# A prompt kernel (state-space convolution and SwiGLU FFN): the buffers of the FFN's inner rows are moved by 64 bytes

## The chip, the cores and the metric

The kernel runs on one core of a Trainium2 chip. The metric is device time of one execution in microseconds. A core has engines that run side by side: PE multiplies matrices (its weight loads are shown as PEld), ACT evaluates functions and copies, DVE and POOL work element by element, SP issues transfers. Each has its own queue of instructions, and semaphores tie the queues together. All operands of PE lie in the core's on-chip memory of 128 partitions; an address below means the byte offset within a partition.

## The reference

The input is a prompt of L = 2048 tokens with D = 448 channels. A conditioning vector gives six rows of scale, shift and gate. Two residual branches follow each other: a diagonal state-space convolution along the tokens, and a SwiGLU FFN with F = 1792 inner rows.

```python
mod = (_silu(c) @ w_mod).reshape(c.shape[0], 6, 1, -1)
sa, ca, ga, sb, cb, gb = ...
h = _layernorm(x) * (1 + ca) + sa
x = x + ga * ssm_conv(h, A, B, C, log_dt, Dskip)
h = _layernorm(x) * (1 + cb) + sb
x = x + gb * ((_silu(h @ w_gate) * (h @ w_up)) @ w_down)
```

Everything is float32, and the FFN is nearly all of the arithmetic: 2048 x 448 x 1792 x 3 products.

## The kernel before

The tokens are 16 tiles of 128. They are handled in six blocks of 2, 2, 3, 3, 3 and 3 tiles (`BLOCKS`). The FFN's inner rows are 14 groups of 128, called `f` in the code. A first stage of about 33 us loads and prepares the six rows, the scan's coefficients and the first two tiles. From then on the FFN of one block runs while the scan and the second normalisation of the next block are worked in between (`TIMES` says at which `f`).

PE multiplies in a one-pass form of float32 that keeps fewer bits. To keep the precision, each operand is split into a high part and a low part, and three products are added: high x high, high x low, low x high. So each tensor of the FFN exists twice: `hhi` and `hlo` for the normalised input (channels on partitions, four slices of the 448 channels), the slices 0 to 6 of `gu` for the gate and up weights, `phi` and `plo` (in the code `hi` and `lo`) for the inner rows, and `wdh` and `wdl` for the down weights.

For one `f`, `gate_up` issues 22 matmuls (line 754): for gate and for up, seven with `hhi` and four with `hlo`. Here a 128 x 128 piece of the weights `gu` is loaded into the array, and `hhi` or `hlo` streams through it, 256 or 384 columns, by the block's number of tiles. ACT makes silu of the gate into a buffer `p` (line 769), DVE multiplies it with the up result (784), ACT copies the product to `phi` (791), and DVE writes what is left of it to `plo` (792).

`down` (line 804) belongs to the `f` before. Here the roles are turned round: a 128 x 128 piece of `phi` or `plo`, one tile of tokens, is the weights that are loaded, and `wdh` or `wdl` streams, 448 columns. For each of three products and each tile of the block there is one matmul: nine with three tiles, six with two. So PE's program is, without end, 22 gate/up matmuls and 9 or 6 down matmuls. Now and then come three matmuls of the scan (lines 976 to 978), which load the triangular matrix `tri` and stream `vh`, `v1` and `vl`, 448 columns too. In the last block the last two inner rows are multiplied in another order (line 832).

Where the buffers lie is set by their order and sizes alone, each pool taking the next free place. The pool `hid` is the last one. It has two buffers of each name, first two of `p`, then of `phi`, then of `plo`, and it ends 224 bytes below the end of the memory. In this layout `hhi`, `hlo`, all `gu`, `wdh`, `wdl`, `p`, `phi` and `plo` start at 32 modulo 256, and `tri` at 128 modulo 256. Their slices keep that, since a slice of 128 columns is 512 bytes, and a row of 448 columns is 7 x 256 bytes. One exception is written into the code: in a block of two tiles, the columns of `hhi` and `hlo` that are used begin at column 48, 192 bytes further on.

```python
first_col = lambda n: 48 if n == 256 else 0
```

Only the first block (`fresh`) takes `p` from the pool `hid`; later blocks use two pieces of a buffer that is free by then (`p_of`).

Of the kernel before, what the change touches and what calls it, by code (L numbers as in the profile page):

```python
# [8 lines left out]
F32 = mybir.dt.float32  # L9
# [42 lines left out]
def f32(ap):  # L52
    return ap.bitcast(F32)
# [3 lines left out]
def tile_kernel(ctx, tc, x, a_re, a_im, b_re, b_im, c_re, c_im, log_dt,  # L57
# [13 lines left out]
    def bank():  # L71
        t = psg.tile([128, 512], F32, name="bank")
        return t
# [26 lines left out]
    p_of = [spare[:, q * 512:q * 512 + MB * 128] for q in range(2)]  # L100
# [11 lines left out]
    def split_d(j, part=None):  # L112
        hi, lo = wp[j]
        if not part:
            sc.copy(hi, wdn[j])
        if part != 0:
            ve.tensor_tensor(lo, wdn[j], f32(hi), op=OP.subtract)

    def split_w(j, part):
        w = raw[j]  # L120
        if part == 0:
            sc.copy(wgu[j][:, :, 0:3, :], w[:, :, 0:3, :])  # L122
            sc.activation(wgu[j][:, :, 3, :], w[:, :, 3, :], AF.Copy, scale=half)  # L123
        else:
            ve.tensor_tensor(wgu[j][:, :, 3:7, :], w[:, :, ::-1, :], f32(wgu[j][:, :, 0:4, :][:, :, ::-1, :]), op=OP.subtract)  # L125
# [604 lines left out]
    def run_blocks(pools, stages, first=None):  # L730
        work, hid = pools.work, pools.hid
        def ffn(ts, fresh, last, todo):
# [4 lines left out]
            def gate_up(f, nw):  # L737
                head = fresh and f < 2
                if fresh and f:
                    split_d(f)  # L740
                w = wgu[f]
                p = hid.tile([128, 256], F32, name="p") if fresh else p_of[f % 2]
                hi = hid.tile([128, MB * 128], F32R, name="phi")
                lo = hid.tile([128, MB * 128], F32R, name="plo")
                ps = [bank(), bank()]

                top = [(k, a) for k, ws in enumerate(((0, 6), (1, 5), (2, 4), (3,))) for a in ws]
                low = [(k, k) for k in range(4)]  # L750

                def mm(s, ka, lo, first=False, end=False):
                    for q, (k, a) in enumerate(ka):
                        pe.matmul(ps[s][:, 0:n], w[:, s, a], (hlo if lo else hhi)[:, k, first_col(n):first_col(n) + n],  # L754
                                  start=first and q == 0, stop=end and q == len(ka) - 1)

                if head:
                    for k in range(3):
                        for s in range(2):
                            mm(s, [(k, k)], False, k == 0)  # L760
                    for s in range(2):
                        mm(s, [(k, 6 - k) for k in range(3)] + [(3, 3)], False)
                    for s in range(2):
                        mm(s, low, True, False, True)
                else:
                    for s in range(2):
                        mm(s, top, False, True)
                        mm(s, low, True, False, True)
                sc.activation(p[:, 0:n], ps[0][:, 0:n], AF.Silu)  # L769
                for g, a in todo.get((f, 2), []):  # L770
                    g(*a)
                pp[f] = hi, lo
                if last and f == NF - 1:
                    c_ = [slice(q * 128, (q + 1) * 128) for q in range(len(ts))]
                    for q in range(len(ts) + 1):
                        for o in c_[q:q + 1]:
                            ve.tensor_tensor(ps[1][:, o], p[:, o], ps[1][:, o], op=OP.mult)  # L777
                            sc.copy(hi[:, o], ps[1][:, o])
                        for o in c_[max(q - 1, 0):q]:
                            ve.tensor_tensor(lo[:, o], ps[1][:, o], f32(hi[:, o]), op=OP.subtract)  # L780
                    return
                if nw is not None:
                    split_w(nw, 0)
                ve.tensor_tensor(ps[1][:, 0:n], p[:, 0:n], ps[1][:, 0:n], op=OP.mult)  # L784
                if fresh and f == 0:
                    split_d(0, 1)
                    for g, a in todo.get("mid", []):
                        g(*a)
                elif nw is not None:
                    split_w(nw, 1)  # L790
                sc.copy(hi[:, 0:n], ps[1][:, 0:n])  # L791
                ve.tensor_tensor(lo[:, 0:n], ps[1][:, 0:n], f32(hi[:, 0:n]), op=OP.subtract)  # L792
                if fresh and f == 0:
                    split_w(nw, 1)
# [52 lines left out]
            for f in range(NF):  # L847
                gate_up(f, f + 2 if fresh and f + 2 < NF else None)
                if fresh:
                    pools.load(f + 2 + NS, f + NS)  # L850
                if last and f in (2, 4):
                    gated(NF - 2 + (f == 4))
                for g, a in todo.get((f, 0), []):
                    g(*a)
                if f and not (last and f == NF - 1):
                    down(f - 1, qz)
                if last and f == NF - 2:
                    last_sums()
                for g, a in todo.get((f, 1), []):
                    g(*a)  # L860
# [250 lines left out]
```

## Time and profile before

| | us |
|---|---|
| median of three runs | 474.72 (474.66 to 474.8) |
| the profiled execution | 474.99 |
| its span, first to last instruction | 473.1 |
| PE busy | 464.2 |
| PEld busy | 439.3 |
| DVE busy | 282.6 |
| ACT busy | 160.1 |
| PE busy in the gate/up matmuls, line 754 (hhi / hlo) | 209.2 / 130.6 |
| PE busy in the down matmuls, line 804 (three products) | 58.0 / 58.1 / 58.2 |

The busy time of matmuls is that of their union: a matmul is shown from its start until its last result is written, the next one starts before that, and the overlap is counted once, for one of them. What a matmul costs on PE is therefore read as the distance from its start to the start of the next, in the timeline. There a row is a run of equal instructions: start, length, engine, line, what it writes and reads, the size of the loaded weights, the size of what streams, and how many. A distance is the difference of two rows' starts divided by the count of the first. Starts are given to 0.01 us, so that a distance over nine matmuls is known to about 1 ns and a single one to 10 ns.

### The profile page before, as it was taken

The numbers are of one execution on the slowest core, as the hardware profiler recorded it, in microseconds if no ns is written. First come the engines' busy times: TensorE is split into PE (matmuls) and PEld (weight loads), VectorE is DVE, ScalarE is ACT, GpSimd is POOL, SyncE is SP. The second block draws the span as 40 slices with busy tenths as digits, with TensorE's granted clock in tenths as the row PEclk, the third lists the DMA queues.
The fourth block names the chain that finished last, engine by engine and source line by source line (L and its number), as shares of the span: only waits on it lengthen the run. The fifth ranks groups of instructions, "written<-read, shape, count | busy, mean of one in ns | idle before, by whom it ended". The sixth has DMA issues, their size and how long they took to land.

```text
span 473.1 us, 7027 instructions
## 1 busy us (share of the span) xinstructions
PE 464.2 (98%) x2735; PEld 439.3 (93%) x2735; DVE 282.6 (60%) x540; ACT 160.1 (34%) x359; POOL 62.4 (13%) x88
## 2 busy tenths in 40 slices
PE   6999999999999999999999999999999999999995
PEld 4669999999999999999999999999999999999995
DVE  5888999778865547573744756464666553222125
ACT  5879566522243122233212233321223222221111
POOL 1222001000000224100022410004141000000000
PEclk9999999999999999999999999999999999999999
DMA  8966652110003000111300011130000112000001
GB/s 307 405 245 183 211 177 92 58 40 2 2 0 99 0 1 0 46 45 46 116 2 0 2 45 46 44 118 1 1 22 24 46 44 79 22 1 1 1 0 64
DMA packets 18779, 31.24 MB, mean 66 GB/s; under 512 B 2608, under 2 KB 13488, under 8 KB 18736
## 3 DMA queue, kind: packets, MB, share of 16 engines
q1 hardware_dynamic: 18096, 30.53, 18.8%
q8 instruction: 23, 0.38, 0.4%
q10 hardware_dynamic: 640, 0.18, 0.2%
q14 instruction: 20, 0.16, 0.1%
HBM read 24.61 MB, written 6.03 MB: 65 GB/s over the span
## 4 chain that ended last, share of the span: by engine, by line
PE 95%; DMA 3%; DVE 1%; ACT 0%; SPq 0%; issue 0%; DVEq 0%
PE bank L754 60%; PE dn L804 28%; DMA wm<-in_w_mod_groups_dram 2%; DMA x<-in_A_u_dram 1%; PE dn L476 1%; PE bank L256 1%; PE bank L977 1%; PE cv L976 1%; PE cv L978 1%; PE bank L266 0%; DVE x L843 0%; PE bank L227 0%; PE bank L394 0%; PE cv L989 0%; PE bank L397 0%; DVE bank L777 0%
## 5 line engine op out<-in xcount | busy, mean ns | idle before, releaser
L754 PE MATMUL bank<-hhi,gu 128*128 128x384 f32 (+1 forms) x1176 | 209.2, 317 | 0.2 <-issue 0.2
L754 PEld LDWEIGHTS bank<-hhi,gu 128*128 128x128 f32 x1176 | 189.8, 188 | 3.8 <-issue 1.0
L754 PE MATMUL bank<-hlo,gu 128*128 128x384 f32 (+1 forms) x672 | 130.6, 316 | 0.0
L754 PEld LDWEIGHTS bank<-hlo,gu 128*128 128x128 f32 x672 | 109.1, 188 | 0.2
L784 DVE TENSOR_TENSOR bank<-raw,bank 128x384 f32<-128x384 f32 (+1 forms) x69 | 36.8, 534 | 121.2 <-PE bank L754 118.5
L791 ACT CAST phi<-bank 128x384 fp32r<-128x384 f32 (+1 forms) x83 | 36.8, 443 | 138.3 <-DVE bank L784 138.2
L769 ACT ACTIVATE raw<-bank 128x384 f32<-128x384 f32 (+1 forms) x70 | 32.9, 470 | 122.7 <-PE bank L754 113.8
L792 DVE TENSOR_TENSOR plo<-bank,phi 128x384 fp32r<-128x384 f32 (+1 forms) x83 | 42.4, 511 | 37.6 <-ACT phi L791 37.5
L804 PE MATMUL dn<-wdh,plo 128*128 128x448 f32 x218 | 58.2, 368 | 0.0
L804 PE MATMUL dn<-wdl,phi 128*128 128x448 f32 x218 | 58.1, 367 | 0.0
L804 PE MATMUL dn<-wdh,phi 128*128 128x448 f32 x218 | 58.0, 367 | 0.0
L804 PEld LDWEIGHTS dn<-wdl,phi 128*128 128x128 f32 x218 | 40.9, 188 | 3.9
L804 PEld LDWEIGHTS dn<-wdh,plo 128*128 128x128 f32 x218 | 40.9, 188 | 3.9
L804 PEld LDWEIGHTS dn<-wdh,phi 128*128 128x128 f32 x218 | 38.5, 188 | 1.1
L185 POOL TENSOR_SCALAR rsb<-mvb 128x1 f32<-128x1 f32 (+2 forms) x13 | 4.6, 354 | 143.6 <-DVE mvb L157 143.6
L125 DVE TENSOR_TENSOR gu<-raw,gu 128x1024 fp32r<-128x1024 f32 x14 | 17.0, 1218 | 1.2 <-ACT gu L123 1.2
L185 POOL TENSOR_SCALAR rsa<-mva 128x3 f32<-128x3 f32 (+1 forms) x6 | 2.3, 380 | 99.3 <-DVE mva L157 97.0
L951 POOL TENSOR_TENSOR m<-m,gm 128x448 f32<-128x448 f32 x9 | 10.4, 1150 | 21.1 <-DVE m L202 17.4
L965 DVE TENSOR_TENSOR vl<-m,vh 128x448 fp32r<-128x448 f32 x12 | 9.0, 754 | 6.7 <-ACT vh L964 6.1
L122 ACT CAST gu<-raw 128x768 fp32r<-128x768 f32 x14 | 11.7, 832 | 0.0
L970 POOL TENSOR_TENSOR m<-m,gd 128x448 f32<-128x448 f32 x9 | 11.5, 1281 | 0.0
L215 ACT ACTIVATE raw<-raw,rsb 128x64 f32<-128x64 f32 x14 | 4.8, 346 | 18.9 <-DVE raw L212 9.7
(243 smaller groups left out, 412.0 us busy)
## 6 DMA issues: line engine op xcount, KB each, us to landing
raw<-in_B_w_gate_up_dram SPq DMA_DIRECT2D x14, 512.0 KB, 3.7
rawd<-in_B_w_down_dram SPq DMA_DIRECT2D x16, 224.0 KB, 3.9
x<-in_A_u_dram SPq DMA_DIRECT2D x12, 224.0 KB, 3.0
out_dram<-x SPq DMA_DIRECT2D x11, 224.0 KB, 1.9
xd<-raw SPq DMA_DIRECT2D x9, 256.0 KB, 2.0
raw<-xd SPq DMA_DIRECT2D x36, 64.0 KB, 2.0
wm<-in_w_mod_groups_dram SPq DMA_DIRECT2D x5, 448.0 KB, 8.2
wm<-in_w_mod_groups_dram SPq DMA_DIRECT2D x5, 336.0 KB, 8.2
```

Source lines behind the costliest of these rows:

```text
L122: sc.copy(wgu[j][:, :, 0:3, :], w[:, :, 0:3, :])
L125: ve.tensor_tensor(wgu[j][:, :, 3:7, :], w[:, :, ::-1, :], f32(wgu[j][:, :, 0:4, :][:, :, ::-1, :]), op=OP.subtract)
L185: po.tensor_scalar(rs[:, 0:n], self.mv[:, 0:n, 1], EPS, None, op0=OP.add)
L754: pe.matmul(ps[s][:, 0:n], w[:, s, a], (hlo if lo else hhi)[:, k, first_col(n):first_col(n) + n], start=first and q == 0, stop=end and q = ...
L769: sc.activation(p[:, 0:n], ps[0][:, 0:n], AF.Silu)
L784: ve.tensor_tensor(ps[1][:, 0:n], p[:, 0:n], ps[1][:, 0:n], op=OP.mult)
L791: sc.copy(hi[:, 0:n], ps[1][:, 0:n])
L792: ve.tensor_tensor(lo[:, 0:n], ps[1][:, 0:n], f32(hi[:, 0:n]), op=OP.subtract)
L804: pe.matmul(dn[q][:, 0:D], u[:, cs], v, start=f == 0 and z == 0, stop=f == (NF - 3 if last else NF - 1) and z == 2)
L951: (ve if on_v else po).tensor_tensor(v, h, g, op=OP.mult)
L965: ve.tensor_tensor(vl, v0, f32(vh), op=OP.subtract)
L970: (ve if on_v else po).tensor_tensor(h, h, gd, op=OP.mult)
```

## The change

In the first block's `gate_up`, the buffer `p` is asked for with 264 columns in place of 256.

```diff
                 w = wgu[f]
-                p = hid.tile([128, 256], F32, name="p") if fresh else p_of[f % 2]
+                p = hid.tile([128, 264], F32, name="p") if fresh else p_of[f % 2]
                 hi = hid.tile([128, MB * 128], F32R, name="phi")
                 lo = hid.tile([128, MB * 128], F32R, name="plo")
```

The additional eight columns are used by nothing. Each of the two buffers `p` grows from 1024 to 1056 bytes, so the second `p` starts 32 bytes later, and the two `phi` and the two `plo` start 64 bytes later: at 96 modulo 256, with `wdh` and `wdl` still at 32. This holds for every block, since `phi` and `plo` are the same buffers throughout. No other buffer moves, and each engine's instructions and waits stand in the same order as before.

## The prediction

> **What bounds the kernel now.** I read the page's busy lines first, then the chain that ended last, then the waits of PE, and only then the timeline of PE at a few places in the middle.
>
> ```profile
> span 473.1 us, 7027 instructions
> PE 464.2 (98%) x2735; PEld 439.3 (93%) x2735; DVE 282.6 (60%) x540; ACT 160.1 (34%) x359; POOL 62.4 (13%) x88
> ...
> PE 95%; DMA 3%; DVE 1%; ACT 0%; SPq 0%; issue 0%; DVEq 0%
> ...
> L804 PE MATMUL dn<-wdh,plo 128*128 128x448 f32 x218 | 58.2, 368 | 0.0
> L804 PE MATMUL dn<-wdl,phi 128*128 128x448 f32 x218 | 58.1, 367 | 0.0
> L804 PE MATMUL dn<-wdh,phi 128*128 128x448 f32 x218 | 58.0, 367 | 0.0
> ```
>
> PE is busy 464.2 of 473.1 us, and 95% of the chain is PE. The down matmuls (L804) are 3 x 218 = 654. The windows by stage say the same more sharply (after the stretch and its length: the busy time of PE, PEld, DVE, ACT and POOL, then the granted clock); the first row is most of the first block, the second the first block of three tiles:
>
> ```profile
> 33.00:85.00 52.00, 52.00 (x383) 49.79 (x384) 49.07 (x88) 37.33 (x87) 5.39 (x10) 1.00 0.49 160
> 141.00:222.00 81.00, 81.00 (x450) 78.74 (x448) 45.19 (x82) 21.65 (x46) 14.69 (x17) 1.00 0.11 35
> ```
>
> PE is busy for 52.00 of 52.00 and for 81.00 of 81.00 us, at the full granted clock of 1.00. So no engine, wait or transfer that feeds PE can shorten it: time there is the number of matmuls times the distance from one start to the next. The mean durations above (367 ns) are not that distance, because matmuls overlap; starts must be read from the timeline.
>
> **How far apart matmuls start.** First a place in a block of three tiles, PE alone:
>
> ```profile
> 198.87 0.78 PE L804 MATMUL dn<-wdh,phi 128*128 128x448 f32 x3
> 199.48 0.78 PE L804 MATMUL dn<-wdl,phi 128*128 128x448 f32 x3
> 200.10 0.78 PE L804 MATMUL dn<-wdh,plo 128*128 128x448 f32 x3
> 200.72 1.38 PE L754 MATMUL bank<-hhi,gu 128*128 128x384 f32 x7
> 201.94 0.85 PE L754 MATMUL bank<-hlo,gu 128*128 128x384 f32 x4
> 202.63 1.20 PE L754 MATMUL bank<-hhi,gu 128*128 128x384 f32 x6
> ```
>
> Nine down matmuls of 448 columns take 200.72 - 198.87 = 1.85 us, 205.6 ns each; the last six 1.24 us, 206.7 ns each. Eleven gate/up matmuls of 384 columns take 202.63 - 200.72 = 1.91 us, 173.6 ns each. Per column that is 0.461 and 0.452 ns. In both, the operand that streams and the weights that are loaded start at equal addresses modulo 256 (all at 32).
>
> Now a block of two tiles, where the streamed `hhi` and `hlo` start 192 bytes further on (column 48), so that the gate/up weights lie 64 bytes behind them modulo 256. This is the relation that the change gives to the down matmuls.
>
> ```profile
> 99.98 0.96 PE L754 MATMUL bank<-hhi,gu 128*128 128x256 f32 x7
> 100.78 0.62 PE L754 MATMUL bank<-hlo,gu 128*128 128x256 f32 x4
> 101.23 0.57 PE L804 MATMUL dn<-wdh,phi 128*128 128x448 f32 x2
> ...
> 102.46 0.97 PE L754 MATMUL bank<-hhi,gu 128*128 128x256 f32 x7
> ...
> 110.53 0.99 PE L754 MATMUL bank<-hhi,gu 128*128 128x256 f32 x7
> 111.36 0.63 PE L754 MATMUL bank<-hlo,gu 128*128 128x256 f32 x4
> 111.83 0.99 PE L754 MATMUL bank<-hhi,gu 128*128 128x256 f32 x7
> ```
>
> Eleven matmuls of 256 columns take 101.23 - 99.98 = 1.25 us, 113.6 ns each, 0.444 ns per column: the cheapest of the three. But the same eleven, at the same addresses, take 111.83 - 110.53 = 1.30 us a little later, 118.2 ns each. So the relation is not all: it also matters at which moment the run of matmuls begins. The six down matmuls take 102.46 - 101.23 = 1.23 us, 205.0 ns each.
>
> Third, the same down matmuls right behind the three small matmuls of the scan:
>
> ```profile
> 204.54 0.36 PE L976 MATMUL cv<-vh,tri 128*128 128x448 f32 x1
> 204.74 0.37 PE L977 MATMUL bank<-v,tri 128*128 128x448 f32 x1
> 204.95 0.36 PE L978 MATMUL cv<-vl,tri 128*128 128x448 f32 x1
> 205.15 0.77 PE L804 MATMUL dn<-wdh,phi 128*128 128x448 f32 x3
> 205.75 0.77 PE L804 MATMUL dn<-wdl,phi 128*128 128x448 f32 x3
> 206.36 0.77 PE L804 MATMUL dn<-wdh,plo 128*128 128x448 f32 x3
> 206.97 1.40 PE L754 MATMUL bank<-hhi,gu 128*128 128x384 f32 x7
> ```
>
> Three scan matmuls, also 448 columns, whose weights `tri` lie 96 bytes behind the streamed operand: 0.61 us, 203 ns each, with single distances of 0.20, 0.21 and 0.20 us. The nine down matmuls then take 206.97 - 205.15 = 1.82 us, 202.2 ns each instead of 205.6, at unchanged addresses. That 206.7 ns is therefore no floor: nothing but the beginning differs, and it is the slowest of the 448-column distances read here.
>
> What could an address have to do with it? The load of the next weights runs while the present matmul streams:
>
> ```profile
> 188.95 0.37 PE L977 MATMUL bank<-v,tri 128*128 128x448 f32 x1
> 188.95 0.19 PEld L978 LDWEIGHTS cv<-vl,tri 128*128 128x128 f32 x1
> 189.16 0.36 PE L978 MATMUL cv<-vl,tri 128*128 128x448 f32 x1
> ...
> 189.35 0.51 PE L754 MATMUL bank<-hhi,gu 128*128 128x384 f32 x2
> ```
>
> The load of L978's weights starts with matmul L977, which streams until L978 begins; L978's own distance to the next start is 0.19 us. Two readers run through memory side by side; with equal addresses both begin at the same place modulo 256. My theory: where they meet, the stream stands still for some ns, and how often they meet hangs on the difference of the addresses and on the moment of the start.
>
> **The change, part by part.** No instruction is added, removed or moved: the order on PE, DVE, ACT, POOL and SP is row for row that of before. (1) Each `p` buffer grows by 32 bytes; the columns used stay. `p` is read and written by ACT and DVE only, in the first block: nothing, since PE is busy all the 52.00 us of that stage. The cover is thin, as DVE has 49.07 us of work there; without it, 4% (the largest swing by address or moment that is shown above) of a DVE instruction's mean of 49.07 / 88 = 0.56 us, for 14 multiplications: 0.3 us. (2) `phi` and `plo` move by 64 bytes. As outputs of ACT and DVE: nothing, same cover. (3) As weights of the down matmuls they now lie 64 bytes behind the streamed `wdh`/`wdl`. This is the only term on the path.
>
> How many distances does (3) touch? A three-tile block has 14 groups of nine, the last block 12 (its last two inner rows are done in line 832), so 3 x 14 + 12 = 54 groups; two blocks of two tiles give 28 groups of six; 54 x 9 + 28 x 6 = 654, the count of the page. Within a group, a distance is that of a streamed `wd` against the next load; eight of nine (five of six) load `phi` or `plo`, the last loads gate/up weights, which have not moved. So 54 x 8 = 432 distances at 205.6 ns and 28 x 5 = 140 at 205.0 ns change.
>
> The new distance is in no row. From below: 190 ns, the 0.19 us of L978; (205.6 - 190) x 432 + (205.0 - 190) x 140 = 8.8 us saved. From above: the swing between two starts of the same eleven matmuls (118.2 against 113.6) is 4%; 4% of 205.6 is 8.2 ns, and 572 x 8.2 = 4.7 us lost. A loss cannot be excluded: equal addresses could as well be the lucky case. Between them I take the row with the same relation, 0.444 ns x 448 = 199 ns. It lies by the scan's 203 (another relation) and the 202.2 (another start). Saved: 432 x 6.6 + 140 x 6.0 = 2.85 + 0.84 = 3.7 us. (4) Left out: the 18 matmuls of line 832 (18 x 6.6 ns = 0.1 us, partly beside waits at the end), and the last gate/up distance ahead of each of the 82 groups, during which the first `phi` is loaded (from 0.452 to 0.444 ns a column is 3 ns, 0.2 us).
>
> (5) Gate/up runs begin at another moment. In three-tile blocks the chain of waits shows what that does:
>
> ```profile
> 200.88 3.82 PE bank L754 x22
> 207.13 3.84 PE bank L754 x22
> ```
>
> The pass behind the ordinary group takes 3.82 us, the one behind the 202.2 ns group 3.84 us: 0.02 x 54 = 1.1 us at most. In two-tile blocks, 22 matmuls cost 2 x 0.05 = 0.10 us more at the slower speed: 28 x 0.10 = 2.8 us at most, nothing if the share of slow passes stays, and a gain if passes that are slow now became fast. I take zero, as both signs are open.
>
> Sum: the profiled execution ran 474.99 us, span 473.1 and 1.9 around it; it stands 0.3 us above the median of 474.72, so differences are carried over as they are: 474.7 - 3.7 = 471.0 us.
>
> The Trainium skill, TensorE: Matmul & The Clock Gate, section "Back-to-back issue gap", gives a warm matmul N / 2.4 + 2.5 ns; by that estimate 448 columns take 189 ns, and if the change removed all that is above it, 572 x 16.5 = 9.4 us would go. By that rule, 471.0 would be 465.3; the trace's 206.7 ns does not agree with it before the change.
>
> **Rivals.** *Nothing happens.* The two reads do not disturb each other and the 206.7 ns has another cause, such as the change of the PSUM bank. For it: steady 173.6 ns for 384 columns for tens of us. Against it: 202.2 and 205.6 ns for the same nine matmuls, 203 ns for others of the same width. It gives 474.7 us. The Trainium skill states it as a rule: in TensorE: Matmul & The Clock Gate, "Step-by-step: what each phase is for", PE has two independent read ports, and loading weights takes no bandwidth from the running matmul. The spread of equal matmuls in this trace speaks against that being all.
>
> *The down matmuls become slower.* One mechanism: with the weights ahead by 64 bytes, the stream, which covers its 1792 bytes while the load covers 512, catches up with it inside the run where before the two met at its very start. Decided by the distance in a group: above 206 ns it is a loss. At half the bound, 210 ns, 572 x 4.1 = 2.3 us: 477.0 us. For it: 118.2 ns at this very relation at one of the two places shown; against it: the level before is already the highest of all.
>
> *The gain is spent in gate/up.* The down groups fall to 202 ns (432 x 3.6 + 140 x 3.0 = 2.0 us saved), but every pass starts at the slow moment: +1.1 + 2.8 us, 476.6 us. It decides once the passes lose more than 2.0 us.
>
> **Numbers.** Down matmuls faster and most of it kept: 0.54. Nothing measurable (within 0.2%, 0.95 us, about what a measurement can tell here): 0.08. Down matmuls slower: 0.26. Gain spent in gate/up: 0.12, nearly all slower. So faster 0.54, same 0.08, slower 0.38. The likeliest case gives 471.0 us; its own range is 467 to 473.5. To leave out no more than 2 in 10, the range runs from 467.5 (7.2 us saved of the 8.8 that the 190 ns bound allows) to 477.5, past the centres of both slower rivals; the bound of 4.7 us lost is left outside.
>
> **What would show it.** In the timeline of a three-tile block: nine down matmuls in about 1.80 us in place of 1.85, with PE still busy through. If they take 1.85, nothing happened; above 1.87, the slower rival. The gate/up pass in the chain: 3.82 right, 3.84 or more the third rival; in two-tile blocks eleven matmuls in 1.25 or 1.30 us. DVE, ACT and the waits should be as before. The prediction is wrong if the distance depends on something finer than 64 bytes, or if the start's moment outweighs the relation.

## The result, and the profile after

The changed kernel takes 474.26 us (median of 22 runs, 473.45 to 475.4); before, measured with it, 475.21 us (22 runs). The ratio is 0.9978, with a 95% interval of 0.9971 to 0.9985: about 1.0 us faster, where 3.7 us were forecast. The profiled execution of the changed kernel ran 474.07 us, its span 472.0 us, against 473.1.

The page and the windows by stage show nothing that would have moved but PE's own matmuls; PE is still busy through, at the full clock. The rows have the columns of the earlier ones:

```profile
PE 463.0 (98%) x2735; PEld 440.2 (93%) x2735; DVE 282.8 (60%) x540; ACT 160.0 (34%) x359; POOL 62.4 (13%) x88
```

```profile
33.00:85.00 52.00, 52.00 (x383) 50.00 (x383) 49.05 (x88) 37.32 (x86) 5.40 (x10) 1.00 0.50 161
141.00:222.00 81.00, 81.00 (x450) 79.08 (x449) 45.18 (x82) 21.52 (x45) 14.69 (x17) 1.00 0.11 35
```

The timeline of PE in a block of three tiles, at the place that the prediction read:

```profile
198.53 0.77 PE L804 MATMUL dn<-wdh,phi 128*128 128x448 f32 x3
199.13 0.77 PE L804 MATMUL dn<-wdl,phi 128*128 128x448 f32 x3
199.74 0.77 PE L804 MATMUL dn<-wdh,plo 128*128 128x448 f32 x3
200.35 1.40 PE L754 MATMUL bank<-hhi,gu 128*128 128x384 f32 x7
201.59 0.85 PE L754 MATMUL bank<-hlo,gu 128*128 128x384 f32 x4
202.28 0.51 PE L754 MATMUL bank<-hhi,gu 128*128 128x384 f32 x2
```

Nine down matmuls take 200.35 - 198.53 = 1.82 us in place of 1.85, so 202.2 ns each in place of 205.6. But the seven gate/up matmuls behind them take 1.24 us, where the same seven took 201.94 - 200.72 = 1.22 us before. The four matmuls behind those take 0.69 us in both (202.28 - 201.59 and 202.63 - 201.94): what is lost in gate/up is lost at the beginning of the pass, and its settled distance, 173 ns, is that of before. The chain that ended last shows both on larger pieces. First before, then after (start, length, what):

```profile
183.24 3.82 PE bank L754 x22
187.06 1.85 PE dn L804 x9
...
189.51 3.84 PE bank L754 x22
193.35 1.85 PE dn L804 x9
195.21 3.82 PE bank L754 x22
```

```profile
194.85 3.84 PE bank L754 x22
198.69 1.82 PE dn L804 x9
200.51 3.84 PE bank L754 x22
204.35 0.20 PE cv L976
204.55 0.21 PE bank L977
204.76 0.20 PE cv L978
204.96 1.82 PE dn L804 x9
206.78 3.82 PE bank L754 x22
```

Before, a pass of 22 gate/up matmuls took 3.82 us, and 3.84 us only behind scan matmuls. After, it takes 3.84 us behind an ordinary group and 3.82 us behind a group that follows the scan: the other way round. Counted over the whole traces by the starts of the matmuls, of 48 passes that nothing else interrupts 39 took 3.82 us before and 42 take 3.84 us after. (Three of the 48 stand directly behind scan matmuls, with no group between; these take 3.84 us in both.) The addresses of gate/up did not change.

In the blocks of two tiles the chain reads, first before, then after:

```profile
97.66 1.23 PE dn L804 x6
98.89 2.51 PE bank L754 x22
101.39 1.23 PE dn L804 x6
102.62 2.51 PE bank L754 x22
```

```profile
97.72 1.21 PE dn L804 x6
98.94 2.51 PE bank L754 x22
101.44 1.21 PE dn L804 x6
102.65 2.59 PE bank L754 x22
```

Groups of six went from 1.23 to 1.21 us. Passes now alternate between 2.51 and 2.59 us. Of 22 passes behind down or scan matmuls, 16 took about 2.51 us before and 11 do after; the others take about 2.59.

Where the time went, as sums of distances from start to start over the whole trace: down matmuls 134.5 to 132.2 us (-2.3), gate/up with three tiles 214.1 to 214.9 (+0.8), with two tiles 72.2 to 72.5 (+0.3). Together -1.2 us; the span fell by 1.1. The first stage varies by itself from one execution to the next: in the traces of this study the first gate/up matmul starts between 32.4 and 34.0 us. From there to the start of the last gate/up matmul, a stretch without that variation, it is 431.0 us before and 430.0 after.

### The profile page after: what moved, and what is told of

It reads as the page before. It is cut to its first block, busy times and chain, and to the rows that moved or that the text cites. A ratio compares the mean times of both kernels' runs of the same rounds, so it can differ in the third digit from the quotient of the medians.

```text
span 472.0 us, 7027 instructions
## 1 busy us (share of the span) xinstructions
PE 463.0 (98%) x2735; PEld 440.2 (93%) x2735; DVE 282.8 (60%) x540; ACT 160.0 (34%) x359; POOL 62.4 (13%) x88
## 4 chain that ended last, share of the span: by engine, by line
PE 95%; DMA 3%; DVE 1%; SPq 0%; ACT 0%; issue 0%; DVEq 0%
PE bank L754 61%; PE dn L804 28%; DMA wm<-in_w_mod_groups_dram 2%; DMA vec<-in_c_log_dt_dram 1%; PE dn L476 1%; PE bank L256 1%; PE bank L977 1%; PE cv L976 1%; PE cv L978 1%; PE bank L266 0%; DVE x L843 0%; PE bank L227 0%; SPq L300 0%; PE cv L989 0%; PE bank L394 0%; PE bank L397 0%
```

## The experiments

**The theories.** A: the distance between two matmuls follows from where the loaded weights lie behind the streamed operand modulo 256, and from the moment at which the run of matmuls starts, which the run before it leaves behind ("64 bytes behind" means that the weights' address less the streamed operand's is 64 modulo 256). B: the place of `p`, which ACT and DVE use, matters. C: the memory has only two kinds of 64 bytes, so that 128 is the same as 0. Beside them stands the prediction's rival that the two reads do not disturb each other, under which nothing should have moved.

**The parts moved without `p`.** An unused tile of 64 bytes stands between `p` and `phi`.

```diff
                 p = hid.tile([128, 256], F32, name="p") if fresh else p_of[f % 2]
+                if fresh and not f:
+                    hid.tile([128, 16], F32, name="gap", bufs=1)
                 hi = hid.tile([128, MB * 128], F32R, name="phi")
```

> phi and plo are moved by 64 bytes with an unused 64-byte tile between p and phi; the buffers p keep their size and place. Theory A (the distance between matmuls follows from where the loaded weights lie behind the streamed operand modulo 256, and from the moment at which a run of matmuls starts): the same times as the change, three-tile groups of nine down matmuls in 1.82 us, the gate/up pass behind them in 3.84 us, the whole about 1 us faster than before (ratio 0.9978 within 0.001). Theory B (the place of p, read and written by ACT and DVE, is what matters): groups of 1.85 us as before, ratio 1.000.

Measured: 474.21 us, ratio 0.9977 (0.9964 to 0.9989), the same as the change. Its chain has groups of 1.82 us and passes of 3.84 us (two lines lower in the code):

```profile
180.81 1.82 PE dn L806 x9
182.62 3.84 PE bank L756 x22
186.47 1.82 PE dn L806 x9
```

**`p` grown and moved, without the parts.** `p` is asked for behind `lo`.

```diff
-                p = hid.tile([128, 256], F32, name="p") if fresh else p_of[f % 2]
                 hi = hid.tile([128, MB * 128], F32R, name="phi")
                 lo = hid.tile([128, MB * 128], F32R, name="plo")
+                p = hid.tile([128, 264], F32, name="p") if fresh else p_of[f % 2]
```

> p is asked for with 264 columns but after phi and plo, so p grows and moves while phi and plo stay at 32 modulo 256 (2048 bytes lower, which is 0 modulo 256). Theory A: the groups of before, 1.85 us, gate/up passes of 3.82 us, ratio 1.000 within 0.001. Theory B: faster by about 1 us as the change.

Measured: ratio 1.000 (0.999 to 1.0009), groups of 1.85 us and passes of 3.82 us; by the starts, 39 and 9 of 48 passes as before. B falls with these two runs. The parts lay 2048 bytes lower here and nothing changed, which agrees with the address counting modulo 256; by itself it would agree with 512, 1024 or 2048 too. Against those speaks that `wdl` lies 1792 bytes behind its `wdh`, 7 x 256 but no multiple of 512, and that matmuls streaming either take the same time in one group (0.61 and 0.62 us for three, in the rows that the prediction shows).

**128 and 192 bytes.** `p` is asked for with 272 and with 280 columns.

> phi and plo lie 128 bytes behind wdh and wdl modulo 256. Theory A: another fixed pattern, groups of nine between 1.78 and 1.86 us that are not 1.82, and a gate/up pass of 3.82 or 3.84 us by the moment at which it starts; the whole between 472 and 476 us. Theory C (the memory is divided into two halves of 64 bytes only, so that 128 is the same as equal addresses): groups of 1.85 us and the time of before, 474.7 us.

> phi and plo lie 192 bytes behind modulo 256, which is 64 bytes ahead. Theory A: a pattern of its own again, groups of nine between 1.78 and 1.88 us; as the stream is the faster reader, weights that lie just ahead of it should be worse than weights just behind, so slower than the change, 474 to 477 us. Theory C: the same as the change, groups of 1.82 us and 474 us.

Measured: 128 bytes 474.98 us, ratio 0.9995 (0.9985 to 1.0006); 192 bytes 472.68 us, ratio 0.9945 (0.9928 to 0.9961). The chain of 128 bytes, then that of 192:

```profile
181.38 1.83 PE dn L804 x9
183.21 3.84 PE bank L754 x22
187.05 1.83 PE dn L804 x9
```

```profile
181.98 1.80 PE dn L804 x9
183.78 3.84 PE bank L754 x22
187.62 1.81 PE dn L804 x9
```

So four offsets give four lengths of a group: 1.85 (equal), 1.82 (64), 1.83 (128) and 1.80 us (192). That 128 came out at the time of before is no proof of C: its groups are 1.83 and its passes 3.84 us, and gain and loss cancel; nor is 192 the same as 64. My expectation for 192, that weights ahead of the stream are worse, was wrong: it is the best. The two readers' order, as I had pictured it, predicts nothing. (The profiled execution of 192 bytes ran 474.14 us, the longest of its four; its first gate/up matmul started 1.2 us later than in the kernel before. From there to the start of the last gate/up matmul it took 428.8 us, 2.2 less than before.)

In all these runs one operand of a pair moves and the other stays. Whether the difference of the two addresses counts, or the place of each one by itself, they can't tell: no run moves both by the same number of bytes.

**The gate/up weights 64 bytes behind in the three-tile blocks.** Two small tiles move from ahead of `hhi` to behind `hlo`, so that `hhi` and `hlo` start at 224 modulo 256 and nothing that is loaded or streamed for the down matmuls moves (`gd`, which POOL reads, moves with them). The two-tile blocks keep their start at 224 by starting at column 0; the three places where the code writes these columns out follow, here and in the next runs, and are left out of the diffs.

```diff
-    ntok = const.tile([128, 1], F32)
-    pick = const.tile([128, 1], F32)
-    first_col = lambda n: 48 if n == 256 else 0
+    first_col = lambda n: 0 if n == 256 else 0
     hhi = const.tile([128, 4, MB * 128], F32R)
     hlo = const.tile([128, 4, MB * 128], F32R)
     gd = const.tile([128, D], F32)
+    pick = const.tile([128, 1], F32)
+    ntok = const.tile([128, 1], F32)
```

> phi and plo as before (equal addresses). Two small tiles are moved behind hhi and hlo, so that in the three-tile blocks the gate/up weights lie 64 bytes behind the streamed hhi and hlo modulo 256; the two-tile blocks keep their start at 224 modulo 256. Theory A (relation and moment): the gate/up matmuls of 384 columns get another fixed distance than 173.3 ns; by the 0.444 ns a column of the two-tile blocks 170 ns, passes of 22 in 3.75 us, 54 x 0.07 = 3.8 us less, about 471 us. Rival (distances that settle at 173.3 ns wherever the run starts mean that 384 columns are at their floor): passes of 3.82 us, 474.7 to 475.2 us. If 64 bytes is worse here, the pass is above 3.86 us.

Measured: 476.58 us, ratio 1.0031 (1.0017 to 1.0044), slower.

```profile
181.62 1.82 PE dn L804 x9
183.44 3.84 PE bank L754 x22
187.29 1.84 PE dn L804 x9
...
189.73 3.89 PE bank L754 x22
```

Neither the 3.75 us of theory A nor the rival's 3.82 us came true. 64 bytes, the relation of the two-tile blocks with their 0.444 ns a column, makes 384 columns dearer (3.84 and 3.89 us in turn, 175 to 177 ns each), not cheaper: by the starts, the three-tile passes cost 2.4 us more in all, of which the down groups, at unchanged addresses, gave back 0.9. So a cost per column can't be carried from one width to another, which is what the prediction had done with 448.

**The same with the parts at 192 bytes; and 128 and 192 bytes for gate/up.** All three ask for `p` with 280 columns, so the parts lie 192 bytes behind. For 128, four small tiles move behind `hlo`; for 192, `sbc` and `flag` move ahead of `hhi`. The two-tile blocks keep their start at 224.

```diff
-    first_col = lambda n: 48 if n == 256 else 0
+    first_col = lambda n: 32 if n == 256 else 0
+    sbc = const.tile([128, 4], F32)
+    flag = const.tile([1, 1], I32)
     hhi = const.tile([128, 4, MB * 128], F32R)
...
-                p = hid.tile([128, 256], F32, name="p") if fresh else p_of[f % 2]
+                p = hid.tile([128, 280], F32, name="p") if fresh else p_of[f % 2]
```

> Gate/up weights 64 bytes behind hhi and hlo, and phi and plo 192 bytes behind wdh and wdl. If the two pairs of buffers are independent terms, groups of nine in 1.80 us as with 192 bytes alone and passes as in the run with the gate/up weights alone; by theory A with 3.75 us passes about 469 us. If the moment at which a run starts outweighs the relation, the two gains don't add up, 471 to 474 us.

> Gate/up weights 128 bytes behind hhi and hlo, phi and plo 192 bytes behind wdh and wdl. Theory A: groups of nine in 1.80 us, passes of another length than 3.84 us, unknown in sign, 3.72 to 3.92 us, 469 to 478 us. Rival (floor at 173.3 ns): passes of 3.82 to 3.84 us, 472.7 us.

> Gate/up weights 192 bytes behind hhi and hlo, phi and plo 192 bytes behind wdh and wdl. Theory A: groups of nine in 1.80 us; as 192 was the best of the four for the down matmuls, passes of 3.72 to 3.82 us, 467 to 472 us. Rival (floor): passes of 3.82 to 3.84 us, 472.7 us.

Measured, as ratios to before: 64 bytes 0.9991 (0.998 to 1.0002); 128 bytes 0.9986 (0.9973 to 0.9999); 192 bytes 0.9925 (0.9908 to 0.9942), 472.05 us. The groups stay at 1.80 to 1.82 us in all three. For 64 bytes, expected at 469 us or at 471 to 474, the 474.91 us measured lie above both, since the passes had been taken for cheaper and are dearer. The passes are 3.88 us for 64 (3.82 behind scan matmuls), 3.86 to 3.87 us for 128, and 3.81 us throughout for 192:

```profile
181.57 1.81 PE dn L804 x9
183.38 3.81 PE bank L754 x22
187.19 1.81 PE dn L804 x9
...
189.60 3.81 PE bank L754 x22
```

This is the fastest kernel of the study, 3.5 us ahead of before and, by the two ratios, about 2.5 us ahead of the change. The rival, that 384 columns are at their floor, holds as far as the best pass of before is hardly undercut (3.81 against 3.82); what is gained is that every pass takes it.

**The change with gate/up at 192 bytes, and gate/up at 192 bytes alone.** As the last diff, with `p` at 264 and at 256 columns.

> The change (phi and plo 64 bytes behind) together with gate/up weights 192 bytes behind hhi and hlo in the three-tile blocks. Theory A, as sharpened by the runs so far (the change's gain in the down groups was given back in the gate/up passes, by where they start; with 192 bytes a pass takes 3.82 us wherever it starts): groups of nine in 1.82 us, passes of 3.82 us, 54 x 0.023 = 1.2 us less than the change alone, ratio to before 0.995. Rival (the change lost elsewhere): the time of the change, ratio 0.998.

> Gate/up weights 192 bytes behind hhi and hlo, phi and plo as before. Theory A: groups of nine in 1.85 us where they start as before, passes of 3.82 us; nearly nothing to gain, since most passes of before take 3.82 us: 0 to 0.6 us less, ratio 0.999 to 1.000. Rival (the relations of the two pairs add up as fixed terms, and the last run's gain over 192 bytes for the parts alone, some 0.6 to 1.2 us, comes back here in full): ratio 0.998.

Measured: 0.9959 (0.9944 to 0.9973) for the change with it, close to the 0.995 expected: with groups of 1.82 and passes of 3.82 us, what the change gave back in the three-tile passes is kept. For gate/up alone I was wrong: 0.9957 (0.9943 to 0.9972), 2.0 us, where 0 to 0.6 us were expected and the rival gave 0.998. Its chain:

```profile
180.88 1.82 PE dn L804 x9
182.70 3.81 PE bank L754 x22
186.51 1.82 PE dn L804 x9
...
188.93 3.81 PE bank L754 x22
```

The down groups fell to 1.82 us although `phi`, `plo`, `wdh` and `wdl` lie at equal addresses as before. Only the run of gate/up matmuls ahead of them is another, and with it the operand that streams while a group's first `phi` is loaded. So the 1.85 us of before is one of at least two lengths that the equal addresses allow, and which one is taken is settled by the run before. Both the changed addresses and another beginning bring 1.82 us, so neither can be booked as a fixed price of its own.

**Two tiles at 192 bytes.** In the fastest kernel, the two-tile blocks start at column 0 as well, 192 bytes in place of 64.

```diff
-    first_col = lambda n: 32 if n == 256 else 0
+    first_col = lambda n: 0
```

> As the fastest run so far (gate/up weights and parts both 192 bytes behind), and the two-tile blocks get 192 bytes for hhi and hlo as well, in place of 64. Theory A: two-tile passes of 22 matmuls get one length of their own, 2.45 to 2.62 us in place of 2.50 and 2.59; the three-tile blocks stay at 1.80 and 3.82 us; the whole 470 to 474.5 us. Rival (two tiles are bound by the load of the weights, not by where they lie): 472.0 us as without it.

Measured: 0.9957 (0.9941 to 0.9973), against 0.9925 without it, measured at another time with its own runs of before. The intervals just touch; the two traces agree with a loss: the two-tile passes cost 2.0 us more, the stretch between the first and the last gate/up matmul 1.7 us more. The rival falls. All two-tile passes take the longer of the two lengths:

```profile
94.92 1.20 PE dn L804 x6
96.13 2.59 PE bank L754 x22
98.72 1.21 PE dn L804 x6
99.93 2.59 PE bank L754 x22
```

So of the offsets tried 192 bytes is best for 448 and for 384 columns, and worse than 64 for 256, where only these two were tried.

**Another moment at unchanged addresses.** The change, with the last down matmul of each group in two halves.

```diff
-                    pe.matmul(dn[q][:, 0:D], u[:, cs], v, start=f == 0 and z == 0, stop=f == (NF - 3 if last else NF - 1) and z == 2)
+                    for c in ((slice(0, 224), slice(224, D)) if (q, z) == (len(ts) - 1, 2) else (slice(0, D),)):
+                        pe.matmul(dn[q][:, c], u[:, cs], v[:, c], start=f == 0 and z == 0,
+                                  stop=f == (NF - 3 if last else NF - 1) and z == 2 and c.stop == D)
```

> The change, with the last down matmul of each group done in two halves of 224 columns, which loads its weights twice. No address moves; only the moment at which the gate/up pass starts. Theory A: the group grows by 10 to 40 ns, and the gate/up pass behind it, at unchanged addresses, no longer takes 3.84 us everywhere but another length, such as 3.82 us. Rival (the addresses alone set the length of a pass): 3.84 us as in the change.

Measured: 476.44 us, ratio 1.0025 (1.0015 to 1.0034).

```profile
181.83 1.83 PE dn L805 x10
183.66 3.86 PE bank L754 x22
187.52 1.83 PE dn L805 x10
...
189.97 3.84 PE bank L754 x22
```

The group grew by 0.01 us only, but the pass behind it went from 3.84 to 3.86 us (not to the 3.82 named as an example), while behind the scan it stays at 3.84. No address moved, so the rival falls: the beginning alone changes the length of a pass.

## Why the prediction was right in sign and wrong in size

*What bounds the kernel*: right. PE is busy throughout, and every gain and loss found is a distance between matmuls.

*Terms (1) and (2), `p` and the outputs of ACT and DVE, nothing*: right. For `p` the run that grew and moved it without the parts shows it. The outputs were not moved apart from the weights, since both are the same buffers; that they cost nothing rests on PE being busy for all of both windows, with the busy time of DVE and ACT as before (49.07 and 49.05, 37.33 and 37.32 us in the first block).

*Term (3), the down distance*: right in sign, too large in size. It was set at 199 ns, from 0.444 ns a column of the two-tile blocks; measured are 202.2 ns in three-tile groups. The prediction had that very number in its own rows, the 202.2 ns of a group behind the scan, and 203 ns of the scan's own matmuls, and passed them over for the row with the same relation. The sum of -3.7 us became -2.3. The step that failed is the carrying of a price per column from 256 to 448 columns: with 384 columns, the same 64 bytes cost 0.3% of the whole. The trace of before could have warned of it: in line 832, by the starts, six matmuls of 256 columns are 0.12 us apart and five of 192 columns 0.11 us, so that a quarter fewer columns save less than a tenth.

*Term (5), gate/up begins at another moment, taken as zero*: wrong, and the second step that failed. It cost 0.8 us with three tiles and 0.3 us with two, +1.1 of the 3.9 us that were named as the most. The row that showed it was quoted (3.84 behind the 202.2 ns group), and it was the better forecast: groups that run at 202 ns are followed by slow passes, in most of the places. To take zero since both signs are open was to set aside the only evidence on the sign. With 202 ns and the three-tile loss, the prediction's own rows give -2.0 + 1.1 = -0.9 us, about what was measured. That this meets the total so closely is in part luck: the terms were -2.3, +0.8 and +0.3 us.

*The rivals*: the third, gain spent in gate/up, happened by half; its loss did not exceed the gain. The second, slower down matmuls, did not occur at any of the three offsets tried. The first, that nothing happens, was wrong: with equal instructions and only addresses moved, the ratios run from 0.9925 to 1.0031. The Trainium skill states in TensorE: Matmul & The Clock Gate, section "Step-by-step: what each phase is for", that PE has two independent read ports and that a load takes no read bandwidth from the running matmul. These one-pass float32 streams can't be forecast by that: nine equal matmuls took 1.85 or 1.80 us by the place of the loaded weights. What happens at the ports no run shows.

*The picture of two readers that meet*: not confirmed. That the distance depends on the addresses and on the run before is shown; that they count modulo 256 agrees with all runs. That the loads and the stream collide in memory remains an inference; the one forecast drawn from it, that weights ahead of the stream are worse, failed at 192 bytes.

## What to carry to other kernels

When PE never idles, read the distance from start to start, not a matmul's duration; it can differ by 1 to 3% between streams of the same instructions, and where the streamed operand and the loaded weights lie (here, in steps of 64 bytes modulo 256) belongs to its causes. Such an offset is to be tried for each width by itself, and judged on all the runs of matmuls that follow it: a gain in one kind of matmul starts the next kind at another moment. A price seen at another moment with the same width was a better forecast than one seen at the same offset with another width.

## What the runs showed of the hardware

- A run of equal matmuls settles into a fixed length of its own, and two lengths can exist at the same addresses: nine times 448 columns in 1.85 or 1.82 us, 22 times 256 columns in 2.51 or 2.59 us. Which is taken is decided by the run before.
- The best of the offsets tried differs by width: of the loaded weights behind the stream, 192 bytes for 448 columns (1.80 us for nine, against 1.85 at equal addresses in the kernel before) and for 384 columns (3.81 us for 22, against 3.84 to 3.89 at 64), but not for 256 (2.59 us, against 2.51 and 2.59 at 64).
- After the change, a slow pass of 22 times 384 columns lost its time in its first matmuls: the first seven took 1.24 us in place of 1.22, the four behind them 0.69 us as before.
- Moving a buffer by 2048 bytes changed no group and no pass; moving it by 64 did.
